# Two linear-attention blocks on one core: exp of q written and mixed in place, two relu buffers, the denominators' sums by two additions, places refitted

## The chip, the cores and the metric

The kernel runs on one core of one Trainium2 chip. A core has a matrix engine (PE, TensorE, with its weight loads PEld), a vector engine (DVE), a scalar engine (ACT), GpSimd (POOL) and SyncE (SP); SP and POOL issue the DMA transfers here. The engines run side by side, each through its own queue of instructions in the order in which the program gives them, and wait for one another by semaphores. The metric is the device time of one execution in microseconds (us); less is better.

## The reference

Two independent blocks, A and B, each on 2048 tokens of width 640 with 32 heads of 20, give their outputs side by side (2048 x 1280). Per block:

```
q, k, v = split(x @ wqkv)
phi(t)  = where(t > 0, t + 1, exp(t)) + 1e-6        # = min(exp(t), 1) + relu(t) + 1e-6
kv  = sum over tokens of phi(k) v^T   (per head)    z = sum over tokens of phi(k)
o   = (phi(q) kv) / (phi(q) z + 1e-6)               # per head
out = o @ wo
```

## The kernel before, in words

Everything is fp32. An fp32 product is made of three matmuls of rounded operands, high x high, high x low and low x high: a tile is *split* into a high part (ACT, a copy that rounds, L182) and a low part (DVE, the difference, L179).

**Phase 1 (to about 285 us)** makes the k half. phi(k) is needed for all tokens; instead of v, the Gram sums of phi(k) with x are formed and v's weights are applied to them afterwards (`kvmm`), and wo is applied to kv (`mmm`, and `m_step` for block B), which gives a matrix M per block so that the output is phi(q) M divided by the denominators. The large products are done in pairs by a scheme with seven products for eight (`product`, `combine`). Each pair has the seven products n = 0 to 6 in PSUM banks: n = 0, 2, 4, 5 use one bank `pa`, n = 1 and 6 `pe`, n = 3 `psb`. Products 2 and 5 add to or overwrite a bank which ACT must first have copied out (`ko<-pa` in phase 1, `o<-pa` in the q half, both L343).

**The q half (about 285 to 564 us)** goes through eight units u of 512 tokens, four per block. In unit u PE first runs `qmm(u, c)` for five chunks c of 128 features, 15 matmuls of 128x512 each into a bank `psq`, and then `outmm(u - 1)`: seven products for each of two halves, 108 matmuls of 128x320. For each chunk `qphi` makes phi(q): exp and relu on ACT (L950, L951), then the mix min(exp, 1) + relu on DVE (L952); `qacc` adds z times phi(q) into `acc`, on ACT for c = 0 and else on DVE (L962). When the chunks of a unit are done, `acc` holds, per token, the products that have to be summed over the rows of a head: `spread` (four SP transfers `da<-acc`) lays four groups of 32 partitions side by side, `invert` sums these four and takes the reciprocal on DVE, `gather` (four SP transfers `rd<-da`) brings it back to all 128 partitions, and `divide` (two halves, DVE, L1003) multiplies phi(q) by it. `d_sums`, `a_split` and `d_split` then make the operands of `outmm(u)` (`da` high and low, `ds` high and low). All this runs while PE works on `qmm(u + 1)`, since `outmm(u)` follows it.

**What sets the order.** Instructions are emitted in an order written by hand. In phase 1 each small piece of work is a job with a spot; `SHIFT` adds a number to a job's spot, and jobs are emitted by their spots. In the q half each piece is put at a slot: `("q", u, c, k)` is the place after the k-th group of three matmuls of chunk c, `("o", u, s)` the place after a product of `outmm(u)`; `AT` moves a piece by so many slots in that list. The high part of a split stands in its slot, and its low part follows one slot later. What is emitted first stands first in its engine's queue, and nothing behind it can pass.

Buffers: `pq` (phi(q) of a unit) has two, `eq` and `rq` one each, `rd` one.

Of the kernel before, what the change touches and what calls it, by code (L numbers as in the profile page):

```python
# [27 lines left out]
    ('fdh', 'k', 1, 6): 0.53, ('fdh', 'm', 0, 6): 0.52, ('fdh', 'm', 0, 7): 0.62, ('fdh', 'm', 0, 8): 0.57, ('fdl',  # L28
# [7 lines left out]
    ('gacc', 0, 1): 3.2, ('gacc', 1, 0): 2.35, ('gacc', 1, 3): 2.05, ('gacc', 2, 1): 2.89, ('gacc', 2, 3): 0.28,  # L36
    ('gacc', 3, 1): 2.86, ('gacc', 3, 2): 2.86, ('gacc', 3, 3): 3.83, ('gacc', 3, 5): 2.14, ('gacc', 4, 0): 0.75,
    ('gacc', 4, 4): 2.17, ('gacc', 5, 3): 1.28, ('gacc', 5, 5): 0.51, ('gacc', 6, 2): 0.82, ('gacc', 7, 0): 0.31,
# [5 lines left out]
    14): 4.05, ('mix', 15): -0.8, ('mix', 17): 1.76, ('mix', 19): 1.66, ('mix', 2): -0.07, ('mix', 20): 0.31,  # L44
    ('mix', 23): 0.53, ('mix', 26): 0.21, ('mix', 29): 2.2, ('mix', 3): -0.55, ('mix', 4): 7.31, ('mix', 5): 7.49,
# [17 lines left out]
    ('relu', 1): 0.93, ('relu', 10): 1.37, ('relu', 11): 0.09, ('relu', 13): 1.06, ('relu', 14): 1.59, ('relu', 21):  # L63
    4.46, ('relu', 25): 2.55, ('relu', 28): 1.48, ('relu', 30): 3.49, ('relu', 5): 1.82, ('s1', 10): -0.46, ('s1',
# [13 lines left out]
    ('woh', 4): -0.51, ('wol', 0): 0.5, ('wol', 3): 0.37, ('wol', 4): 0.03, ('wqh', 1): 2.01, ('wql', 2): -0.55,  # L78
# [43 lines left out]
def tile_linear_attn_pair(ctx: ExitStack, tc: tile.TileContext, ins, out: bass.AP):  # L122
# [863 lines left out]
    def invert(u):  # L986
        t = acc[u]
        nc.vector.tensor_reduce(t[:, 1, :P], t[:, 0].rearrange("p (j s) -> p s j", j=4),
                                axis=mybir.AxisListType.X, op=OP.add)
        nc.vector.reciprocal(t[:, 1, P:2 * P], t[:, 1, :P])  # L990
# [608 lines left out]
```

## Time and profile before

| what | value |
|---|---|
| median of 3 runs | 573.01 us (571.81 to 573.55) |
| the profiled execution's own time | 568.97 us |
| its span, first to last instruction | 567.2 us |
| granted TensorE clock | 1.000 |
| busy: PE, DVE, ACT, POOL | 559.9, 426.2, 329.9, 84.6 us |

A row of the timeline has the start in us, the duration, the engine, the line, the operation, out<-in by the program's names, the shapes, a count, and in brackets the time for which the engine stood idle before it and what ended that. A row of a group of instructions has the summed busy time and the mean ns of one, then the idle time of the engine before them. Matmuls are pipelined: the steps between their starts are the pace, and their durations overlap. A row of the waits has the total in us, the number of times and the longest.

### The profile page before, as it was taken

What the parts mean: (1) busy time and instruction counts of PE and PEld (TensorE: products, weight loads), DVE (VectorE), ACT (ScalarE), POOL (GpSimd) and SP (SyncE); (2) the same over time, 40 slices, a digit from 0 to 9 for tenths busy, and PEclk for the clock granted to TensorE, in tenths of its full rate; (3) what the DMA queues carried; (4) which work ended last, traced back from release to release, by engine and by line L of the source; (5) the groups of instructions that cost most, each with busy time, mean ns of one, the idle gap of its engine ahead of it and who ended that gap; (6) DMA issues with size and microseconds to landing.
All of it is one profiled execution on the core that took longest, in us unless ns stands there. A gap on an engine that the chain in (4) does not pass through costs nothing.

```text
span 567.2 us, 9114 instructions
## 1 busy us (share of the span) xinstructions
PE 559.9 (99%) x3231; PEld 511.5 (90%) x3231; DVE 426.2 (75%) x723; ACT 329.9 (58%) x619; POOL 84.6 (15%) x141
## 2 busy tenths in 40 slices
PE   8999999999999999999999999999999999999997
PEld 7989999898999898989888899898989989898997
DVE  5977799886585778887836895968679485776792
ACT  5964676663675775665736754646547354454551
POOL 0111122311011211242200103110012101001010
PEclk9999999999999999999999999999999999999999
DMA  8868689999885887999998976746466994432022
GB/s 281 242 155 245 169 239 298 288 315 356 304 206 141 199 259 135 353 226 297 319 266 282 333 249 237 253 130 215 153 214 226 305 366 145 155 94 102 1 94 92
DMA packets 78613, 126.74 MB, mean 223 GB/s; under 512 B 9768, under 2 KB 40872, under 8 KB 78568
## 3 DMA queue, kind: packets, MB, share of 16 engines
q1 hardware_dynamic: 66120, 86.28, 47.0%
q0 software_dynamic: 12160, 39.66, 25.6%
q8 instruction: 25, 0.41, 0.3%
q10 hardware_dynamic: 288, 0.23, 0.1%
q14 instruction: 20, 0.16, 0.1%
HBM read 73.62 MB, written 49.37 MB: 217 GB/s over the span
## 4 chain that ended last, share of the span: by engine, by line
PE 92%; DVE 3%; DMA 2%; ACT 1%; issue 0%; SPq 0%; ACTq 0%; DVEq 0%
PE pa L339 22%; PE pe L339 10%; PE psg L190 8%; PE psg L191 8%; PE psg L189 8%; PE psq L189 7%; PE psq L190 7%; PE psq L191 7%; PE psb L339 7%; PE psk L600 4%; PE pskv L782 2%; DMA wst<-in_A_wk 1%; DMA rd<-da 1%; PE psm L189 1%; PE psm L190 1%; PE psm L191 1%
## 5 line engine op out<-in xcount | busy, mean ns | idle before, releaser
L189 PE MATMUL psq<-xqh,wqh 128*128 128x512 f32 x200 | 78.4, 392 | 0.0
L191 PE MATMUL psq<-xqh,wql 128*128 128x512 f32 x200 | 78.0, 390 | 0.0
L190 PE MATMUL psq<-xql,wqh 128*128 128x512 f32 x200 | 77.9, 389 | 0.0
L189 PE MATMUL psg<-pkh,xnh 128*128 128x512 f32 x160 | 62.8, 393 | 0.0
L191 PE MATMUL psg<-pkh,xnl 128*128 128x512 f32 x160 | 62.7, 392 | 0.0
L190 PE MATMUL psg<-pkl,xnh 128*128 128x512 f32 x160 | 62.6, 392 | 0.0
L343 ACT ACTIVATE o<-pa 128x320 f32<-128x320 f32 x64 | 27.6, 440 | 49.7 <-PE pa L339 49.6
L567 POOL DMA_DIRECT2D zd<-ek x30 | 26.2, 873 | 140.1 <-DVE ek L559 50.1
L191 PEld LDWEIGHTS psq<-xqh,wql 128*128 128x128 f32 x200 | 37.5, 188 | 8.0
L190 PEld LDWEIGHTS psq<-xql,wqh 128*128 128x128 f32 x200 | 37.6, 188 | 7.3
L189 PEld LDWEIGHTS psq<-xqh,wqh 128*128 128x128 f32 x200 | 37.6, 188 | 7.2
L950 ACT ACTIVATE eq<-psq 128x512 f32<-128x512 f32 x40 | 23.8, 594 | 34.7 <-PE psq L191 26.2
L343 ACT ACTIVATE ko<-pa 128x320 f32<-128x320 f32 x52 | 22.5, 434 | 36.8 <-PE pa L339 36.6
L952 DVE SCALAR_TENSOR_TENSOR pq<-eq,rq 128x512 f32<-128x512 f32 x40 | 27.5, 688 | 12.4 <-ACT rq L951 12.2
L191 PEld LDWEIGHTS psg<-pkh,xnl 128*128 128x128 f32 x160 | 30.0, 188 | 6.5 <-DVE xnl L179 0.2
L1003 DVE SCALAR_TENSOR_TENSOR pq<-pq,rd 128x1280 f32<-128x1280 f32 x16 | 23.5, 1483 | 16.0 <-DMA rd<-da 16.0
L190 PEld LDWEIGHTS psg<-pkl,xnh 128*128 128x128 f32 x160 | 30.0, 188 | 5.8 <-DVE pkl L575 0.4
L189 PEld LDWEIGHTS psg<-pkh,xnh 128*128 128x128 f32 x160 | 30.0, 188 | 5.2
L571 ACT ACTIVATE pkh<-ek,epst 128x640 fp32r<-128x640 f32 x32 | 26.4, 832 | 11.5 <-DVE ek L559 11.4
L559 DVE SCALAR_TENSOR_TENSOR ek<-ek,ko 128x640 f32<-128x640 f32 x32 | 26.2, 820 | 7.8 <-ACT ko L556 6.8
L645 DVE TENSOR_TENSOR gacc<-psg,gacc 128x512 f32<-128x512 f32 (+2 forms) x42 | 25.6, 627 | 6.8 <-PE psg L191 6.5
L575 DVE SCALAR_TENSOR_TENSOR pkl<-ek,pkh 128x640 fp32r<-128x640 f32 x32 | 25.9, 819 | 6.0 <-ACT pkh L571 6.0
(212 smaller groups left out, 1657.7 us busy)
## 6 DMA issues: line engine op xcount, KB each, us to landing
zd<-ek POOLq DMA_DIRECT2D x32, 320.0 KB, 5.3
out<-o POOLq DMA_DIRECT2D x28, 320.0 KB, 3.6
xql<-xd SPq DMA_DIRECT2D x24, 256.0 KB, 4.0
xt<-in_B_xt_tiles SPq DMA_DIRECT2D x16, 320.0 KB, 5.0
xn<-in_B_x SPq DMA_DIRECT2D x16, 320.0 KB, 5.7
xqs<-in_A_xt SPq DMA_DIRECT2D x20, 256.0 KB, 5.8
xqs<-in_B_xt SPq DMA_DIRECT2D x20, 256.0 KB, 6.2
fdmh<-fsh POOLq DMA_DIRECT2D x14, 320.0 KB, 4.5
```

The costliest lines, as they stand in the source:

```text
L189: nc.tensor.matmul(o, whi, xhi, start=first, stop=False)
L190: nc.tensor.matmul(o, whi, xlo, start=False, stop=False)
L191: nc.tensor.matmul(o, wlo, xhi, start=False, stop=last)
L339: nc.tensor.matmul(o, x, y, start=start and m == r == 0, stop=m == len(terms) - 1 and r == 2, skip_group_check=True)
L343: nc.scalar.activation(x, y, AF.Copy)
L559: nc.vector.scalar_tensor_tensor(ek[n], ek[n], 1.0, rk[n], op0=OP.min, op1=OP.add)
L567: nc.gpsimd.dma_start(zacc[b], e, accum_op=OP.add)
L571: nc.scalar.activation(pk[n][0], ek[n], AF.Identity, bias=epst)
L575: nc.vector.scalar_tensor_tensor(lo, ek[n], EPS, f32(hi), op0=OP.add, op1=OP.subtract)
L645: nc.vector.tensor_tensor(o, x, o, op=OP.add)
L950: nc.scalar.activation(e, ps, AF.Exp)
L952: nc.vector.scalar_tensor_tensor(pq[u][:, c, :], e, 1.0, r, op0=OP.min, op1=OP.add)
```

## The change

Three edits in the code and two in its tables of places.

- `qphi`: exp writes into the chunk of `pq` itself and the mix works there in place; the tile `eq` is gone. `rq` has two buffers. So the exp of a chunk waits no longer for the mix of the chunk before it, which read `eq`; the relu waits for the mix two chunks back.
- `invert`: the reduction over four columns becomes two additions, of 256 and of 128 columns. The reciprocal is the same; `gather` reads it from another place of the same tile.
- `AT` is written anew: about half of its entries have other values, some are new, some gone. From `SHIFT` 24 entries are taken out, so that these jobs go back to the spots that they have without it (among them ('mix', 17), the mix of a token group of phase 1).

```
 SHIFT = {
...
-    14): 4.05, ('mix', 15): -0.8, ('mix', 17): 1.76, ('mix', 19): 1.66, ('mix', 2): -0.07, ('mix', 20): 0.31,
...
+    14): 4.05, ('mix', 15): -0.8, ('mix', 19): 1.66, ('mix', 2): -0.07, ('mix', 20): 0.31, ('mix', 23): 0.53,
...
 AT = {
-    ('a_split', 1, 0): 3, ('a_split', 2, 0): 3, ('a_split', 3, 0): -1, ('a_split', 3, 1): 2, ('a_split', 5, 0): -2,
...
+    ('d_split', 1, 0): 7, ('d_split', 1, 1): 5, ('d_split', 3, 1): -5, ('d_sums', 1, 0): 4, ('divide', 1, 0): 1,
...
+    'm', 1, 2): -3, ('form_split', 'm', 1, 3): -11, ('form_split', 'm', 1, 8): 3, ('form_split', 'm', 1, 9): 5,
+    ('form_sums1', 'm', 1, 1): -5, ('gather', 5): 4, ('invert', 3): -1, ('invert', 5): 3, ('kv_step', 1, 5): -2,
+    ('load_w', 'q', 1, 0): -3, ('load_w', 'q', 1, 4): 8, ('m_step', 1, 2): 1, ('m_step', 1, 3): 1, ('split_o', 1,
...
     def qphi(u, c, ps):
...
-        e = q2[0].tile([P, 512], F32, name="eq", tag="eq", bufs=1)
-        r = q1a[0].tile([P, 512], F32, name="rq", tag="rq", bufs=1)
+        e = pq[u][:, c, :]
+        r = q1a[0].tile([P, 512], F32, name="rq", tag="rq", bufs=2)
         nc.scalar.activation(e, ps, AF.Exp)
         nc.scalar.activation(r, ps, AF.Relu)
-        nc.vector.scalar_tensor_tensor(pq[u][:, c, :], e, 1.0, r, op0=OP.min, op1=OP.add)
+        nc.vector.scalar_tensor_tensor(e, e, 1.0, r, op0=OP.min, op1=OP.add)
...
     def invert(u):
         t = acc[u]
-        nc.vector.tensor_reduce(t[:, 1, :P], t[:, 0].rearrange("p (j s) -> p s j", j=4),
-                                axis=mybir.AxisListType.X, op=OP.add)
-        nc.vector.reciprocal(t[:, 1, P:2 * P], t[:, 1, :P])
+        tt = nc.vector.tensor_tensor
+        tt(t[:, 1, :2 * P], t[:, 0, :2 * P], t[:, 0, 2 * P:], op=OP.add)
+        tt(t[:, 1, 2 * P:3 * P], t[:, 1, :P], t[:, 1, P:2 * P], op=OP.add)
+        nc.vector.reciprocal(t[:, 1, 3 * P:], t[:, 1, 2 * P:3 * P])
...
     def gather(u):
...
-            nc.sync.dma_start(r[32 * j:32 * (j + 1), :], t[:, 1, P:2 * P])
+            nc.sync.dma_start(r[32 * j:32 * (j + 1), :], t[:, 1, 3 * P:])
```

The line numbers of the changed kernel are 5 or 6 lower than before.

The order of DVE in unit 2, from the last operation on z (`zs`) to the first low part `dsl` that `outmm(1)` reads, and beyond; before:

```order
L751 TENSOR_SCALAR zs<-zs 128x1
L179 TENSOR_TENSOR dsl<-sr,dsh 128x1024
L179 TENSOR_TENSOR fsl<-wst,fsh 128x640
L952 SCALAR_TENSOR_TENSOR pq<-eq,rq 128x512
L962 SCALAR_TENSOR_TENSOR acc<-pq,z,acc 128x512
L179 TENSOR_TENSOR dal<-pq,dah 128x768
L179 TENSOR_TENSOR dal<-pq,dah 128x256
```

and after the change:

```order
L745 TENSOR_SCALAR zs<-zs 128x1
L173 TENSOR_TENSOR fsl<-wst,fsh 128x640
L946 SCALAR_TENSOR_TENSOR pq<-pq,rq 128x512
L956 SCALAR_TENSOR_TENSOR acc<-pq,z,acc 128x512
L173 TENSOR_TENSOR dal<-pq,dah 128x768
L173 TENSOR_TENSOR dal<-pq,dah 128x256
L173 TENSOR_TENSOR dsl<-sr,dsh 128x1024
```

The first `dsl` has moved behind a weight's low part, a mix, an accumulation and the second `dal`.

The order of ACT in the same unit, from the exp of the fourth chunk to the first copies out of the product bank; before:

```order
L950 ACTIVATE eq<-psq 128x512
L951 ACTIVATE rq<-psq 128x512
L886 ACTIVATE fsh<-wst 128x640
L182 ACTIVATE dsh<-sr 128x1024
L950 ACTIVATE eq<-psq 128x512
L951 ACTIVATE rq<-psq 128x512
L343 ACTIVATE o<-pa 128x320 x3
```

and after the change:

```order
L944 ACTIVATE pq<-psq 128x512
L945 ACTIVATE rq<-psq 128x512
L176 ACTIVATE dsh<-sr 128x1024
L944 ACTIVATE pq<-psq 128x512
L945 ACTIVATE rq<-psq 128x512
L337 ACTIVATE o<-pa 128x320
L880 ACTIVATE fsh<-wst 128x640
L337 ACTIVATE o<-pa 128x320 x2
```

The rounding of a weight (`fsh`) has moved from between the last two exps to behind the first copy.

In phase 1, ACT at about 153 us, where block A's tenth pair of products is on PE and the first `kvmm` steps stand between its products; before:

```order
L343 ACTIVATE ko<-pa 128x320
L547 ACTIVATE ek<-ko 128x640
L556 ACTIVATE ko<-ko 128x640
L435 ACTIVATE kah<-xt 128x512
L343 ACTIVATE ko<-pa 128x320
L571 ACTIVATE pkh<-ek,epst 128x640
```

and after the change:

```order
L337 ACTIVATE ko<-pa 128x320
L565 ACTIVATE pkh<-ek,epst 128x640
L541 ACTIVATE ek<-ko 128x640
L550 ACTIVATE ko<-ko 128x640
L429 ACTIVATE kah<-xt 128x512
L337 ACTIVATE ko<-pa 128x320
```

`pkh`, which reads what the mix (17) has written, now stands ahead of the exp, the relu, the rounding and the second copy out of `pa`. On DVE that mix has moved ahead of two low parts of x (`xnl`).

More of the change, by code (lines that the diff above doesn't have):

```diff
@@ L27 @@
     0, 0): 0.42, ('f5', 'k', 0): -0.1, ('f5', 'k', 1): -2.28, ('fdh', 'k', 1, 2): 0.51, ('fdh', 'k', 1, 4): 0.91,
-    ('fdh', 'k', 1, 6): 0.53, ('fdh', 'm', 0, 6): 0.52, ('fdh', 'm', 0, 7): 0.62, ('fdh', 'm', 0, 8): 0.57, ('fdl',
[7 rows of a table removed]
-    ('gacc', 0, 1): 3.2, ('gacc', 1, 0): 2.35, ('gacc', 1, 3): 2.05, ('gacc', 2, 1): 2.89, ('gacc', 2, 3): 0.28,
-    ('gacc', 3, 1): 2.86, ('gacc', 3, 2): 2.86, ('gacc', 3, 3): 3.83, ('gacc', 3, 5): 2.14, ('gacc', 4, 0): 0.75,
-    ('gacc', 4, 4): 2.17, ('gacc', 5, 3): 1.28, ('gacc', 5, 5): 0.51, ('gacc', 6, 2): 0.82, ('gacc', 7, 0): 0.31,
+    ('fdh', 'k', 1, 6): 0.53, ('fdh', 'm', 0, 7): 0.62, ('fdh', 'm', 0, 8): 0.57, ('fdl', 'k', 1, 1): 0.84, ('fdl',
[6 rows of a table added]
+    ('fl', 'm', 0, 8): 1.99, ('gacc', 0, 1): 3.2, ('gacc', 1, 0): 2.35, ('gacc', 1, 3): 2.05, ('gacc', 2, 1): 2.89,
+    ('gacc', 2, 3): 0.28, ('gacc', 3, 1): 2.86, ('gacc', 3, 2): 2.86, ('gacc', 3, 3): 3.83, ('gacc', 3, 5): 2.14,
+    ('gacc', 4, 0): 0.75, ('gacc', 4, 4): 2.17, ('gacc', 5, 3): 1.28, ('gacc', 5, 5): 0.51, ('gacc', 7, 0): 0.31,
     ('gacc', 7, 1): 0.04, ('gacc', 7, 4): 0.45, ('gacc', 7, 5): 1.7, ('gacc', 7, 6): 2.69, ('iota', 0): 0.8, ('kt',
@@ L43 @@
     ('ld', 'm', 0, 4): -0.19, ('mc', 4, 1): 0.69, ('mix', 11): 0.24, ('mix', 12): 0.49, ('mix', 13): 7.61, ('mix',
-    14): 4.05, ('mix', 15): -0.8, ('mix', 17): 1.76, ('mix', 19): 1.66, ('mix', 2): -0.07, ('mix', 20): 0.31,
-    ('mix', 23): 0.53, ('mix', 26): 0.21, ('mix', 29): 2.2, ('mix', 3): -0.55, ('mix', 4): 7.31, ('mix', 5): 7.49,
[17 rows of a table removed]
-    ('relu', 1): 0.93, ('relu', 10): 1.37, ('relu', 11): 0.09, ('relu', 13): 1.06, ('relu', 14): 1.59, ('relu', 21):
-    4.46, ('relu', 25): 2.55, ('relu', 28): 1.48, ('relu', 30): 3.49, ('relu', 5): 1.82, ('s1', 10): -0.46, ('s1',
[13 rows of a table removed]
-    ('woh', 4): -0.51, ('wol', 0): 0.5, ('wol', 3): 0.37, ('wol', 4): 0.03, ('wqh', 1): 2.01, ('wql', 2): -0.55,
[19 rows of a table removed]
+    14): 4.05, ('mix', 15): -0.8, ('mix', 19): 1.66, ('mix', 2): -0.07, ('mix', 20): 0.31, ('mix', 23): 0.53,
+    ('mix', 26): 0.21, ('mix', 29): 2.2, ('mix', 3): -0.55, ('mix', 5): 7.49, ('mix', 7): 1.18, ('mix', 8): 4.49,
[16 rows of a table added]
+    11): 0.09, ('relu', 13): 1.06, ('relu', 21): 4.46, ('relu', 25): 2.55, ('relu', 28): 1.48, ('relu', 30): 3.49,
[13 rows of a table added]
+    ('wol', 4): 0.03, ('wqh', 1): 2.01, ('wql', 2): -0.55, ('wql', 4): 2.4, ('xh', 10, 'A1'): -0.17, ('xh', 10,
[17 rows of a table added]
 }
@@ L106 @@
 AT = {
-    ('a_split', 1, 0): 3, ('a_split', 2, 0): 3, ('a_split', 3, 0): -1, ('a_split', 3, 1): 2, ('a_split', 5, 0): -2,
-    ('a_split', 6, 0): 6, ('d_split', 1, 1): 5, ('d_split', 2, 1): -2, ('d_split', 5, 0): 2, ('d_split', 5, 1): 5,
-    ('d_sums', 1, 0): 3, ('d_sums', 3, 0): 1, ('d_sums', 5, 0): -1, ('divide', 1, 0): 1, ('divide', 1, 1): 1,
-    ('divide', 2, 0): 3, ('divide', 2, 1): 2, ('form_last', 'm', 1): 2, ('form_split', 'm', 1, 0): 2, ('form_split',
-    'm', 1, 1): -2, ('form_split', 'm', 1, 2): -1, ('form_split', 'm', 1, 3): -4, ('form_split', 'm', 1, 5): -5,
-    ('form_split', 'm', 1, 8): 2, ('form_split', 'm', 1, 9): 4, ('form_sums1', 'm', 1, 1): -6, ('gather', 6): 3,
-    ('invert', 3): -1, ('invert', 6): -4, ('kv_step', 1, 2): 1, ('kv_step', 1, 5): -2, ('load_w', 'q', 1, 4): 9,
-    ('m_step', 1, 3): 1, ('split_o', 1, 4): -1, ('split_w', 1, 0): -3, ('split_w', 1, 2): -10, ('split_w', 1, 4): 2,
-    ('z_turn', 1): 2,
+    ('a_split', 1, 0): 2, ('a_split', 2, 0): -1, ('a_split', 3, 0): -1, ('a_split', 5, 0): 2, ('a_split', 6, 0): 7,
+    ('d_split', 1, 0): 7, ('d_split', 1, 1): 5, ('d_split', 3, 1): -5, ('d_sums', 1, 0): 4, ('divide', 1, 0): 1,
+    ('divide', 2, 0): 1, ('divide', 5, 0): 1, ('form_last', 'm', 1): 5, ('form_load', 0, 5): -2, ('form_load', 1,
+    1): -2, ('form_load', 1, 5): -1, ('form_split', 'm', 1, 0): 5, ('form_split', 'm', 1, 1): -4, ('form_split',
+    'm', 1, 2): -3, ('form_split', 'm', 1, 3): -11, ('form_split', 'm', 1, 8): 3, ('form_split', 'm', 1, 9): 5,
+    ('form_sums1', 'm', 1, 1): -5, ('gather', 5): 4, ('invert', 3): -1, ('invert', 5): 3, ('kv_step', 1, 5): -2,
+    ('load_w', 'q', 1, 0): -3, ('load_w', 'q', 1, 4): 8, ('m_step', 1, 2): 1, ('m_step', 1, 3): 1, ('split_o', 1,
+    5): -2, ('split_w', 1, 0): -3, ('split_w', 1, 2): -7, ('split_w', 1, 4): 1,
 }
```

108 rows, old and new, of the table SHIFT are left out of this document.

## The prediction

> **What bounds the kernel now.** I read the page's first part first: busy time by engine.
>
> ```profile
> PE 559.9 (99%) x3231; PEld 511.5 (90%) x3231; DVE 426.2 (75%) x723; ACT 329.9 (58%) x619; POOL 84.6 (15%) x141
> ```
>
> PE is busy for 559.9 of 567.2 us. The change takes no matmul away, so it can win only where PE stands still or runs slower than its pace. Second view: the waits of PE, and beside them the one kind of wait of ACT that the new tile and buffers touch (us in total, times, longest).
>
> ```profile
> PE pa L339 <- ACT o L343: 2.0, 2, 1.0
> ```
>
> ```profile
> ACT eq L950 <- DVE pq L952: 7.0, 8, 1.8
> ```
>
> Two waits of PE, 2.0 us together, are for ACT's copy of a half product (`o<-pa`): the third product of outmm writes a bank that is free only when the first product has been copied out of it. And ACT waits 7.0 us in eight places until the mix has read `eq`. Third view: the instructions of PE at these two waits.
>
> ```profile
> 364.53 0.40 PE L191 MATMUL psq<-xqh,wql 128*128 128x512 f32 x1
> 364.77 0.31 PE L339 MATMUL pa<-fh,dah 128*128 128x320 f32 x1
> ...
> 368.14 0.31 PE L339 MATMUL pe<-fh,dsl 128*128 128x320 f32 x1
> 369.48 0.41 PE L339 MATMUL pa<-fh,dsh 128*128 128x320 f32 x1 [1.03 <-ACT o L343]
> ```
>
> ```profile
> 468.07 0.31 PE L339 MATMUL pe<-fh,dsl 128*128 128x320 f32 x1
> 469.32 0.42 PE L339 MATMUL pa<-fh,dsh 128*128 128x320 f32 x1 [0.94 <-ACT o L343]
> ```
>
> From 364.77 to 368.14 are 24 matmuls, 23 steps: 3.37 / 23 = 0.147 us each. The step to 369.48 is 1.34, so 1.19 is lost, and the matmul after the wait takes 0.41 instead of 0.31, another 0.10: **1.29 us** at unit 2. By the same sum unit 5 loses 1.25 - 0.147 + 0.10 = **1.20 us**. These 2.49 us are what can be won in the q half. From the copy's start to the matmul that it frees I take 0.50 in both places (368.98 to 369.48, 468.82 to 469.32, rows below).
>
> **Part 1: exp into pq, two buffers for relu.** ACT's rows ahead of the two late copies:
>
> ```profile
> 365.42 0.60 ACT L950 ACTIVATE eq<-psq 128x512 f32<-128x512 f32 x1 [1.82 <-DVE pq L952]
> ...
> 368.01 0.60 ACT L950 ACTIVATE eq<-psq 128x512 f32<-128x512 f32 x1
> ...
> 368.98 0.78 ACT L343 ACTIVATE o<-pa 128x320 f32<-128x320 f32 x2
> ```
>
> ```profile
> 462.73 0.60 ACT L950 ACTIVATE eq<-psq 128x512 f32<-128x512 f32 x1 [1.25 <-DVE pq L952]
> ...
> 465.69 0.60 ACT L950 ACTIVATE eq<-psq 128x512 f32<-128x512 f32 x1
> ...
> 467.85 0.60 ACT L950 ACTIVATE eq<-psq 128x512 f32<-128x512 f32 x1 [1.07 <-DVE pq L952]
> ...
> 468.82 0.77 ACT L343 ACTIVATE o<-pa 128x320 f32<-128x320 f32 x2
> ```
>
> In time, the copy must start 0.50 ahead of the step that PE would take: at 368.14 + 0.15 - 0.50 = 367.79 in unit 2, and at 467.72 in unit 5. It starts 0.97 after the last exp (368.01 to 368.98), with the relu between.
>
> Unit 5: if nothing but the wait of 1.07 goes, the last exp starts at 466.78 and the copy at 467.75, on the edge. The wait of 1.25 ahead of it goes too, since ACT then waits only for the mix two chunks back, so 1.2 us come on top. Gain **1.20**, the whole stall; what bounds it is 1.10 (edge missed by a little) to 1.20.
>
> Unit 2: the wait of 1.82 goes, and the weight rounding (`fsh`) that stood between the last two exps is now behind the copy, as the order shows. The last exp then starts when its bank is full, after the matmul of 364.53 has ended at 364.93; say 364.97. Copy at 365.94, 1.85 ahead of its time. Gain **1.29**, if the next operand is there (part 3). Costs: no instruction is added. A mix that writes where it reads needs a price; the nearest rows are operations of the k half of the same shapes, one in place and one not.
>
> ```profile
> L559 DVE SCALAR_TENSOR_TENSOR ek<-ek,ko 128x640 f32<-128x640 f32 x32 | 26.2, 820 | 7.8 <-ACT ko L556 6.8
> ...
> L575 DVE SCALAR_TENSOR_TENSOR pkl<-ek,pkh 128x640 fp32r<-128x640 f32 x32 | 25.9, 819 | 6.0 <-ACT pkh L571 6.0
> ```
>
> 820 and 819 ns: in place costs nothing. The rest of the eight waits, 2.9 of the 7.0 us, stands where no copy is late, or chunks ahead of a copy; it gives nothing by itself.
>
> **Part 2: the sums of the denominators.** The groups that price it, and the one taken away:
>
> ```profile
> L453 DVE TENSOR_TENSOR sx<-sx,xt 128x256 f32<-128x256 f32 x13 | 5.5, 426 | 0.4
> ...
> L179 DVE TENSOR_TENSOR kal<-xt,kah 128x128 fp32r<-128x128 f32 x16 | 4.5, 283 | 0.0
> ```
>
> ```profile
> L988 DVE TENSOR_REDUCE da<-da 128x128 f32<-128x512 f32 x6 | 6.5, 1085 | 5.5 <-DMA da<-acc 5.5
> ```
>
> One 1.085 is replaced by 0.426 + 0.283 = 0.71, with one more handing on between dependent instructions, some 0.04: 0.33 us less, six times. The Trainium skill ("VectorE: DVE Perf Modes", Rules for kernel authors) says to keep the number of DVE operations down, since each pays for emptying the pipe; its formula for the fp32 add, (N + 151) / 0.96 ns, gives 0.42 and 0.29 us, which the rows bear out, and also 0.16 us for the fixed part, so that by the rule alone, with as many elements read, the pair would be 0.16 slower and not 0.33 faster, and the sum at the end -1.1 instead of -1.6. The row of the reduction, twice as long as four operands of 128 take, decides for the pair. The 0.33 is worth nothing by itself: DVE idles in every unit until `rd` lands. It counts through the landing only, in unit 2.
>
> **Part 3: the places in unit 2.** DVE there:
>
> ```profile
> 353.08 2.90 DVE L1003 SCALAR_TENSOR_TENSOR pq<-pq,rd 128x1280 f32<-128x1280 f32 x2 [3.93 <-DMA rd<-da]
> ...
> 360.69 0.69 DVE L952 SCALAR_TENSOR_TENSOR pq<-eq,rq 128x512 f32<-128x512 f32 x1
> 361.41 0.75 DVE L962 SCALAR_TENSOR_TENSOR acc<-pq,z,acc 128x512 f32<-128x512 f32 x1
> 362.08 0.18 DVE L747 TENSOR_REDUCE z<-zr 128x5 f32<-128x20 f32 x1
> ...
> 362.77 1.22 DVE L179 TENSOR_TENSOR dsl<-sr,dsh 128x1024 fp32r<-128x1024 f32 x1
> 363.90 0.82 DVE L179 TENSOR_TENSOR fsl<-wst,fsh 128x640 fp32r<-128x640 f32 x1
> 364.64 0.69 DVE L952 SCALAR_TENSOR_TENSOR pq<-eq,rq 128x512 f32<-128x512 f32 x1
> ...
> 366.03 1.29 DVE L179 TENSOR_TENSOR dal<-pq,dah 128x768 fp32r<-128x768 f32 x2
> 367.23 0.68 DVE L952 SCALAR_TENSOR_TENSOR pq<-eq,rq 128x512 f32<-128x512 f32 x1
> ```
>
> ```profile
> 366.68 0.19 PEld L339 LDWEIGHTS pe<-fh,dsl 128*128 128x128 f32 x1
> ```
>
> From the divide on, DVE works without a gap. The first `dsl` is done at 363.99 and wanted by PE's weight load at 366.68. Afterwards four things stand ahead of it: `fsl` (363.90 to 364.64: 0.74), a mix (360.69 to 361.41: 0.72), an accumulation (361.41 to 362.08: 0.67) and two `dal` (366.03 to 367.23: 1.20), 3.33 together. It starts at 362.77 + 3.33 = 366.10 and ends at 367.32. With the divide 0.33 sooner: 366.99, and PE loads at 367.02: 0.34 late, and 0.10 for the slow first matmul. **Loss 0.44**. Bounds: 0 (`rd` lands 0.7 sooner) and 0.77 (the 0.33 does not pass through the transfers). I take 0.44 because the gather is issued as soon as the reciprocal is done, so that an earlier end is an earlier issue.
>
> In the other units I followed both queues in the same way: the first copy is there 1.4 to 1.8 us ahead of need, since exp and relu of the last chunk (0.97) are all that stands between the full bank and the copy, and `dsl` 2 us ahead or more. The places of `invert` and `gather` in units 5 to 7 move the landing of `rd` by up to 1 us inside that margin: nothing. SP's queue keeps its sequence in the q half but for two pairs of loads that swap. The step of M that now stands behind three more matmuls (`m_step`, 1, 2) adds none: nothing.
>
> **Part 4: phase 1, without 24 shifts.** Most of them put an instruction before or after a neighbour with a wide margin. One place has a narrow one, at 153 to 157 us, where `pkh` now stands ahead of an exp, a relu, a `kah` and the copy that PE's sixth product waits for:
>
> ```profile
> 152.73 0.82 DVE L179 TENSOR_TENSOR xnl<-xn,xnh 128x640 fp32r<-128x640 f32 x1
> ```
>
> ```profile
> 153.54 0.73 ACT L547 ACTIVATE ek<-ko 128x640 f32<-128x640 f32 x1
> 154.30 0.74 ACT L556 ACTIVATE ko<-ko 128x640 f32<-128x640 f32 x1
> 154.95 0.62 ACT L435 ACTIVATE kah<-xt 128x512 fp32r<-128x512 f32 x1
> 155.59 0.44 ACT L343 ACTIVATE ko<-pa 128x320 f32<-128x320 f32 x1
> 155.92 0.82 ACT L571 ACTIVATE pkh<-ek,epst 128x640 fp32r<-128x640 f32 x1
> 156.64 0.29 ACT L795 ACTIVATE kvh<-kvt 120x120 fp32r<-120x120 f32 x1
> ```
>
> ```profile
> 156.36 0.39 PE L339 MATMUL pa<-wfh,kah 128*128 128x320 f32 x1
> ```
>
> The mix takes the place of `xnl` at 152.73 and is done at 153.55; `pkh` starts at 153.58, 0.04 after the exp's old start, and takes 0.72 (155.92 to 156.64). So all behind it comes 0.76 later, the copy at 156.35, the matmul at 156.85 instead of 156.36: **loss 0.49**. Bounds: 0 (if ACT is earlier here) and 0.9 (0.76 and a slow first matmul, no slack).
>
> **Sum:** -1.29 - 1.20 + 0.44 + 0.49 = **-1.56 us** against the profiled execution's 568.97. The median of the runs is 573.01, 4.0 longer; I let that distance stand: 573.01 - 1.56 = 571.4, or -0.27%. What a measurement of this kernel can tell from no change is about 0.3%, 1.7 us, so that this forecast lies at the edge.
>
> **Rivals.** (a) The two new waits don't come: `rd` of unit 2 lands sooner, and ACT has slack at 154. For it: the landing of `rd` varies, and in unit 2, where DVE waits 3.93 for it, it is one of the slow ones (the view of the tile `rd`, 24 transfers, us from issue to landing, min, median, max):
>
> ```profile
> DMA to landing us min/median/max: 2.2/2.7/5.0
> ```
>
> Then -2.49 or, where the runs lose more at these stalls than the profile shows, -3.5: 570.5 to 569.5. (b) In unit 2 the wait for the copy is only exchanged for one for `dsl`: DVE's row is full from 353.08 on, and every us that `rd` comes later counts whole. One us later: -1.56 + 1.0, 572.4. Against it: 5.0 is already the slowest landing. (c) Slower: the same late `dsl`, decided by the landing of `rd`. The stores of split weights at that time go out in another sequence, and if these fill the DMA engines in the few us after `invert`, `rd` waits behind them; from 3.3 us later on, the whole is slower by over 0.3% (3.6: 575.0). The median landing of 2.7 and the maximum of 5.0 speak against it. To this I count a place of phase 1 that I priced at nothing.
>
> **How the numbers follow.** The forecast has 0.60, and with 0.5 us for the runs' own spread a little under half of it lies beyond -0.3%; (a) 0.20, (b) 0.08, (c) 0.12. Faster: 0.28 + 0.20 = 0.48; same: 0.32 + 0.08 = 0.40; slower 0.12. The range goes from (a) with its larger loss, 569.5, to both new waits at their bounds (-2.49 + 0.77 + 1.0 for an `rd` one us late + 0.9 = +0.18) and 0.5 for the spread, 573.7.
>
> **What would show it.** After the change PE has no wait for `o<-pa` of over 0.1 us, and ACT none for the mix in units 2 and 5. PE waits about 0.3 us for `dsl` in the first `pe` product of unit 2, and its step at 156 us is about 0.5 longer. The pair of additions starts 0.79 us ahead of the reciprocal. The prediction is wrong if a wait for `o<-pa` stays, if `rd` of unit 2 lands over a us from 352.7, or if PE stands still in phase 1 anywhere else than before.

## The result

| | before | after |
|---|---|---|
| median of 9 runs each | 571.81 us (569.91 to 574.63) | 567.85 us (566.94 to 569.45) |
| ratio, 95% interval | | 0.993 [0.9905, 0.9956] |
| the profiled execution's own time | 568.97 us | 567.32 us |
| its span | 567.2 us | 565.2 us |

The change makes the kernel 0.7% faster. The direction was forecast, the size not: 571.4 us stood against a median of 573.01, a ratio of 0.997, with a range down to 569.5. On another chip the medians of the same two kernels lie 3.4 us apart (570.87 and 567.46). The two profiled executions lie only 1.65 us apart (2.0 in span), the medians 4.0. How that can be is the main question below.

The waits of PE after the change (total in us, times, longest), the whole answer of that view:

```profile
PE psi L1111 <- DVE idle L1108: 1.0, 1, 1.0
PE pa L333 <- ACT mev L337: 0.7, 1, 0.7
```

Both waits for `o<-pa` are gone, and no wait at all is left in the q half. The place in unit 2 where PE stood for 1.03 us at 369.48, on PE and ACT after the change:

```profile
368.68 0.31 PE L333 MATMUL pe<-fh,dsl 128*128 128x320 f32 x1
368.83 0.31 PE L333 MATMUL pa<-fh,dsh 128*128 128x320 f32 x1
```

```profile
365.51 0.60 ACT L944 ACTIVATE pq<-psq 128x512 f32<-128x512 f32 x1 [1.23 <-PE psq L185]
366.00 0.59 ACT L945 ACTIVATE rq<-psq 128x512 f32<-128x512 f32 x1
366.48 0.44 ACT L337 ACTIVATE o<-pa 128x320 f32<-128x320 f32 x1
```

The step is 0.15, the pace. The last exp now waits for its bank to be filled (PE) and no longer for a mix (DVE), and the copy follows 0.97 behind it, as worked out. DVE and the weight load that were to be late:

```profile
352.51 2.89 DVE L998 SCALAR_TENSOR_TENSOR pq<-pq,rd 128x1280 f32<-128x1280 f32 x2 [2.80 <-DMA rd<-da]
...
365.53 1.22 DVE L173 TENSOR_TENSOR dsl<-sr,dsh 128x1024 fp32r<-128x1024 f32 x1
```

```profile
367.22 0.19 PEld L333 LDWEIGHTS pe<-fh,dsl 128*128 128x128 f32 x1
```

`dsl` is done at 366.75 and loaded at 367.22: 0.47 in hand instead of 0.34 late. The sums on DVE:

```profile
344.42 0.41 DVE L983 TENSOR_TENSOR da<-da 128x256 f32<-128x256 f32 x1
344.86 0.29 DVE L984 TENSOR_TENSOR da<-da 128x128 f32<-128x128 f32 x1
345.19 0.95 DVE L985 RECIPROCAL da<-da 128x128 f32<-128x128 f32 x1
```

The reciprocal starts 0.77 behind the first addition; 1.12 it was behind the reduction. And the place of phase 1 that the prediction priced:

```profile
155.22 1.21 PE L776 MATMUL pskv<-gacc,wv 128*120 128x120 f32 x10
156.54 0.41 PE L333 MATMUL pa<-wfh,kah 128*128 128x320 f32 x1
```

From the ten small matmuls to the sixth product it takes 1.32 now; before it was 0.98 (155.38 to 156.36).

### The profile page after: what moved, and what is told of

Its sections match the earlier page's. It is cut to its first block, busy times and chain, and to the rows that moved or that the text cites. A ratio compares the mean times of both kernels' runs of the same rounds, so it can differ in the third digit from the quotient of the medians.

```text
span 565.2 us, 9089 instructions
## 1 busy us (share of the span) xinstructions
PE 560.1 (99%) x3231; PEld 512.0 (91%) x3231; DVE 423.8 (75%) x729; ACT 329.5 (58%) x619; POOL 84.4 (15%) x141
## 4 chain that ended last, share of the span: by engine, by line
PE 96%; ACT 1%; DMA 1%; issue 0%; DVE 0%; POOL 0%; DVEq 0%; ACTq 0%
PE pa L333 22%; PE pe L333 11%; PE psq L183 8%; PE psq L185 8%; PE psq L184 8%; PE psg L184 8%; PE psg L185 8%; PE psg L183 8%; PE psb L333 7%; PE psk L594 5%; PE pskv L776 2%; DMA md<-mev 1%; PE psi L1111 1%; PE psm L183 1%; PE psm L185 1%; PE psm L184 1%
## 5 line engine op out<-in xcount | busy, mean ns | idle before, releaser
L944 ACT ACTIVATE pq<-psq 128x512 f32<-128x512 f32 x40 | 23.7, 594 | 28.0 <-PE psq L185 27.8
L946 DVE SCALAR_TENSOR_TENSOR pq<-pq,rq 128x512 f32<-128x512 f32 x40 | 27.4, 686 | 8.4 <-ACT rq L945 8.4
L340 DVE TENSOR_TENSOR o<-pe,o 128x320 f32<-128x320 f32 x32 | 15.3, 479 | 20.4 <-PE pe L333 13.5
```

What stands on the lines that cost most here:

```text
L944: nc.scalar.activation(e, ps, AF.Exp)
L946: nc.vector.scalar_tensor_tensor(e, e, 1.0, r, op0=OP.min, op1=OP.add)
```

## The experiments

Theories at the start. **A**: the kernel before loses a varying time at the copies out of the product bank, because the landing of `rd` varies; the in-place exp alone takes that away. **B**: the extra length of its runs lies elsewhere. **C**: the new places gain. After the first runs came **D** (edits and new places are both needed), **F** (the two edits of the code together are enough) and **G** (the denominators make a loop from unit to unit). All ratios are to the kernel before on the same chip, with 95% intervals.

**The kernel before, another execution of it.** No edit.

> The kernel before, unchanged, for another profiled execution of it. Theory A (the kernel before loses a varying time at the copies out of the product bank, because the landing of rd varies and the exps wait for the mixes): this profile differs from the first; PE's waits for o<-pa sum to something other than 2.0 us, and where the execution is longer than 568.97 by x us, these waits are longer by most of x, with rd landing later in the units concerned. Theory B (the extra length of the runs lies elsewhere: the start, the end, phase 1): the waits for o<-pa stay at 2.0 +-0.3 us and the difference stands at other lines. Ratio to the kernel before: 1.000 within its interval.

Ratio 1.0006 [0.9989, 1.0023]. The profiled execution took 570.86 us, 1.89 more than the first, near the median of its runs (570.73). Its wait of PE for the copies, and the one that the first execution did not have:

```profile
PE pa L339 <- ACT o L343: 2.6, 3, 1.1
```

```profile
436.18 0.31 PE L339 MATMUL pe<-fh,dsl 128*128 128x320 f32 x1
437.31 0.41 PE L339 MATMUL pa<-fh,dsh 128*128 128x320 f32 x1 [0.82 <-ACT o L343]
```

This is unit 4. The exp ahead of that copy had been released by PE in the first execution; in this one, 2.1 us later, it is released by a mix (first execution, then this one):

```profile
433.76 0.60 ACT L950 ACTIVATE eq<-psq 128x512 f32<-128x512 f32 x1 [1.29 <-PE pa L339]
```

```profile
435.84 0.60 ACT L950 ACTIVATE eq<-psq 128x512 f32<-128x512 f32 x1 [1.29 <-DVE pq L952]
```

By the steps between the starts of PE's matmuls (0.147 for 320 columns, 0.227 for 512, all that is over the pace added up), this execution loses 3.4 us in the q half, the first one 2.5. The other 1 us lies in phase 1: PE's first `psq` matmul, the start of the q half, stands at 286.04 in the first execution and at 286.98 in this one. So theory A holds for half of the difference and B for the other half, and the first profile was an execution with little waiting.

**Exp in place and two relu buffers alone**, all places and the reduction as before:

```
-        e = q2[0].tile([P, 512], F32, name="eq", tag="eq", bufs=1)
-        r = q1a[0].tile([P, 512], F32, name="rq", tag="rq", bufs=1)
+        e = pq[u][:, c, :]
+        r = q1a[0].tile([P, 512], F32, name="rq", tag="rq", bufs=2)
...
-        nc.vector.scalar_tensor_tensor(pq[u][:, c, :], e, 1.0, r, op0=OP.min, op1=OP.add)
+        nc.vector.scalar_tensor_tensor(e, e, 1.0, r, op0=OP.min, op1=OP.add)
```

> The kernel before with one edit: exp into pq, mix in place, two buffers for relu; all places and the reduction as before. Theory A: both waits for o<-pa are gone, since the last exp no longer waits for a mix; profiled PE time lost falls by about 2.5 us, and the runs gain as much as the whole change or nearly: -3 to -4 us (0.993 to 0.995). Theory C (the new places are what gains): -1 us or less (0.998 to 1.000).

Ratio 1.0002 [0.998, 1.0024]: nothing that can be measured. Two of the twelve executions weigh on this ratio: 575.20 and 572.50 us, with a mean granted clock of 0.994 and 0.997. The medians alone (569.65 against 570.31) give 0.9988, 0.7 us. The waits for `o<-pa` are gone as theory A says, and another has come, twice:

```profile
PE pe L339 <- DVE o L346: 2.1, 2, 1.0
```

The first of them, on DVE and on PE:

```profile
409.86 1.09 DVE L988 TENSOR_REDUCE da<-da 128x128 f32<-128x512 f32 x1 [2.98 <-DMA da<-acc]
410.98 0.95 DVE L990 RECIPROCAL da<-da 128x128 f32<-128x128 f32 x1
411.85 0.43 DVE L346 TENSOR_TENSOR o<-pe,o 128x320 f32<-128x320 f32 x1
```

```profile
410.99 0.31 PE L339 MATMUL pa<-f,dal 128*128 128x320 f32 x1
412.33 0.41 PE L339 MATMUL pe<-fh,dsh 128*128 128x320 f32 x1 [1.04 <-DVE o L346]
```

The seventh product of outmm writes the bank `pe`, which the addition `o<-pe` must first have read. That addition stands in DVE's queue behind the sum of the denominators, and the sum waits 2.98 us for `da` to land. PE loses 1.19 in that step, and again at 447.82 in the next unit. The forecast of theory A falls: the time won at the copies is given back there. The reason is in one more row of each kernel, the divide that runs during unit 3 (of unit 2's phi(q)); before, then with the exp in place:

```profile
383.52 2.90 DVE L1003 SCALAR_TENSOR_TENSOR pq<-pq,rd 128x1280 f32<-128x1280 f32 x2 [0.92 <-DMA rd<-da]
```

```profile
383.46 2.89 DVE L1003 SCALAR_TENSOR_TENSOR pq<-pq,rd 128x1280 f32<-128x1280 f32 x2 [1.86 <-DMA rd<-da]
```

PE is 1.0 us further in the second one (the last `psq` matmul of unit 3 starts at 397.69, before at 398.69), `rd` is not. The denominators go round once per unit: `da` lands, sum, `rd` lands, divide, DVE's queue of the unit, `acc`, `da` again. Where this loop is late, it stops PE at one or the other of the two waits.

**The changed kernel with the old qphi** (the four lines above turned back in the changed kernel):

> The changed kernel with the eq tile and one relu buffer back (old qphi), additions and all new places kept. Theory A: waits for o<-pa in units 2 and 5 come back, 1 to 3 us in sum, and the runs stand at -1 to +1 us against the kernel before (0.998 to 1.002). Theory C: -3 us or more (0.995 or below).

Ratio 1.001 [0.9989, 1.0032]. The wait for `o<-pa` is back, not in units 2 and 5 as expected but in one place, unit 4:

```profile
435.22 0.31 PE L333 MATMUL pe<-fh,dsl 128*128 128x320 f32 x1
437.81 0.46 PE L333 MATMUL pa<-fh,dsh 128*128 128x320 f32 x1 [2.28 <-ACT o L337]
```

Ahead of the copy stands an exp that has waited 2.64 us for a mix:

```profile
436.34 0.60 ACT L944 ACTIVATE eq<-psq 128x512 f32<-128x512 f32 x1 [2.64 <-DVE pq L946]
```

This execution, 572.24 us, is the second longest of twelve (median 569.78), and it pays for more than the wait. The granted clock reads 0.80 from 435 to 440 us, 0.85 from 440 to 445, and 1.00 before and after. From 437.81 to 441.50 there are 14 steps of 0.26 us on the average, where the pace is 0.147: another 1.6 us. Theory C falls: additions and new places without the in-place exp gain nothing.

**The additions alone:**

```
-        nc.vector.tensor_reduce(t[:, 1, :P], t[:, 0].rearrange("p (j s) -> p s j", j=4),
-                                axis=mybir.AxisListType.X, op=OP.add)
-        nc.vector.reciprocal(t[:, 1, P:2 * P], t[:, 1, :P])
+        tt = nc.vector.tensor_tensor
+        tt(t[:, 1, :2 * P], t[:, 0, :2 * P], t[:, 0, 2 * P:], op=OP.add)
+        tt(t[:, 1, 2 * P:3 * P], t[:, 1, :P], t[:, 1, P:2 * P], op=OP.add)
+        nc.vector.reciprocal(t[:, 1, 3 * P:], t[:, 1, 2 * P:3 * P])
...
-            nc.sync.dma_start(r[32 * j:32 * (j + 1), :], t[:, 1, P:2 * P])
+            nc.sync.dma_start(r[32 * j:32 * (j + 1), :], t[:, 1, 3 * P:])
```

> The kernel before with one edit: the two additions in place of the reduction. By the prediction's own rows the divide of units 2 and 5 starts 0.33 us sooner, so that both late copies are 0.33 us less late: -0.6 to -0.7 us (0.999). If the landing of rd is set by other transfers and not by its issue, 0.

Ratio 1.0004 [0.9989, 1.002]. In the profile the two late copies are less late, by about as much as forecast:

```profile
PE pa L339 <- ACT o L343: 1.4, 2, 0.7
```

1.4 instead of 2.0. The runs cannot tell 0.6 us from nothing.

**The changed kernel itself, again:**

> The changed kernel itself, for its ratio on this chip and a second profiled execution: 0.993 (0.9905 to 0.9956 before). No wait of PE for o<-pa or o<-pe of over 0.3 us in the q half.

Ratio 0.9937 [0.9915, 0.9958]; its second profile (567.07 us) has no wait in the q half either.

**The changed kernel with the old AT table:** the whole table `AT` as before, both edits kept.

> The changed kernel with the places of the q half (AT) as before the change; both edits of the code and the shortened SHIFT kept. Theory D (two waits hang on the late denominators: the exp for the mix, and PE's sixth bank for the o<-pe addition which stands behind the sums that wait for da; the in-place exp takes the first away, the places the second): the second wait stays, at 409 to 412 or 443 to 448 us, 1 to 2.5 us in all, and the runs stand at 0.998 to 1.001. Theory F (the two edits of the code together are the gain): 0.993 to 0.995.

Ratio 0.9944 [0.9926, 0.9963], no wait in the q half. Theory D falls and F stands: the refitted places, the larger part of the diff, are worth nothing that can be measured. In the traces they do one thing that the prediction did not see. PE wants `dsl` of unit 2 behind a longer queue with the new `AT`, but `rd` of unit 2 lands sooner with it. From the first issue of `rd` to the divide it takes 7.12 to 7.22 us in all ten profiles with the old `AT`, and 6.27 to 6.39 in all five with the new one; SP's rows of the kernel before and of the changed kernel, whose divides start at 353.08 and 352.51:

```profile
345.93 2.59 SPq L996 DMA_DIRECT2D rd<-da  x4
```

```profile
346.17 2.59 SPq L991 DMA_DIRECT2D rd<-da  x4
```

The stores that POOL issues at that time stand in another sequence with the new `AT`; that this is the cause was not tested. A trace of use in the times there may be: 5 of these 12 runs lie at 568.65 to 568.90, the other 7 at 566.64 to 567.40, while the 8 runs of the changed kernel beside them end at 568.13; but the changed kernel's first runs reached 569.45, so that this use is not shown.

**The changed kernel with the old SHIFT table:** all 24 entries back.

> The changed kernel with the whole SHIFT of before. By the prediction the wait at 156 us goes (0.3 us less than in the changed kernel) and nothing else moves: 0.992 to 0.994. If the 24 entries carry the gain: 0.996 or more.

Ratio 0.9931 [0.9906, 0.9955]: no difference from the changed kernel, as expected. The wait at 156 us is gone, but the wait for `mev` at 196 us is 1.0 in its profile, where the two of the changed kernel have 0.7 and 0.5.

**Exp in place, and the sums of units 3 and 4 put behind the additions** (on the kernel before with exp in place; of `AT` the entries that change):

```
+    ('gather', 3): 2, ('gather', 4): 2,
-    ('invert', 3): -1,
+    ('invert', 3): 2, ('invert', 4): 2,
```

> The kernel before with exp in place and two relu buffers, and the sums of the denominators of units 3 and 4 (with their gathers) moved two or three places, behind the two o<-pe additions of the fifth product. Theory D: the two waits of PE for o<-pe of the run with exp in place alone (1.0 each) are gone, no wait for o<-pa returns, and the runs gain 2 to 3 us: 0.994 to 0.997. If the late da or rd is only handed on, a wait of about 1 us turns up elsewhere: 0.998 to 1.000.

Ratio 0.994 [0.9917, 0.9963], and the q half has no wait. Nothing is made shorter here; the addition `o<-pe` only no longer stands behind an instruction that waits for a transfer:

```profile
409.27 0.49 DVE L346 TENSOR_TENSOR o<-pe,o 128x320 f32<-128x320 f32 x1
409.68 1.07 DVE L988 TENSOR_REDUCE da<-da 128x128 f32<-128x512 f32 x1
```

**Both edits of the code, every place as before** (the two diffs above together on the kernel before):

> The kernel before with both edits of the code (exp in place with two relu buffers, and the two additions), every place of before. Theory G (the denominators make a loop from unit to unit: da lands, sums, rd lands, divide, DVE's queue of the next unit, acc, da again; PE waits where this loop runs late, and the edits each shorten it by a few tenths up to the point where no wait is left): no wait for o<-pa, and the waits for o<-pe of the run with exp in place alone are gone or under 0.7 us in all; 0.994 to 0.996. If the additions' 0.33 us count only for themselves: two waits of about 0.7 stay, 0.998 to 0.999.

Ratio 0.9948 [0.9933, 0.9963]. So the additions, worth nothing alone, are worth about 3 us on top of the exp in place (1.0002 to 0.9948). The profiled execution was one of the two longest of six (568.46) and has one wait left for `o<-pe`, 0.36 us at 446.92. Against the run with the exp alone, unit 3 reads (exp alone, then both):

```profile
397.69 0.40 PE L191 MATMUL psq<-xqh,wql 128*128 128x512 f32 x1
```

```profile
403.84 1.26 SPq L983 DMA_DIRECT2D da<-acc  x2
```

```profile
398.76 0.40 PE L191 MATMUL psq<-xqh,wql 128*128 128x512 f32 x1
```

```profile
404.17 1.26 SPq L983 DMA_DIRECT2D da<-acc  x2
```

```profile
409.42 0.43 DVE L989 TENSOR_TENSOR da<-da 128x256 f32<-128x256 f32 x1 [1.48 <-DMA da<-acc]
```

Measured from PE's last `psq` matmul, the first `da` is issued 0.74 sooner (5.41 behind it instead of 6.15), the sums start 5.25 after that instead of 6.02, 0.77 less, and they take 0.33 less up to the addition `o<-pe`: 1.84 us against the 1.19 that the seventh product was late. Of these, 0.33 is the edit itself; the 0.74 fits the loop, where a unit's start inherits what the unit before saved: the divide during unit 3 already starts 0.71 sooner against that matmul (383.82 against 398.76, 383.46 against 397.69); for the landing no cause is shown.

**Exp in place, and unit 3's da ahead of the xql loads** (on the kernel before with exp in place). SP issues the five loads of the next unit's low parts of x in front of the four `da` transfers; here behind them (the new entries of `AT`):

```
+    ('load_xq', 4, 0): 7, ('load_xq', 4, 1): 6, ('load_xq', 4, 2): 5, ('load_xq', 4, 3): 4, ('load_xq', 4, 4): 3,
```

> The kernel before with exp in place and two relu buffers, and unit 3's four da transfers issued ahead of the five xql loads of the next unit on SP's queue (these loads moved 3 to 7 places back); the order on DVE, ACT and PE is that of the run with exp in place alone, except that nothing else moves. Theory G: da of unit 3 lands 2 us or more sooner than at 409.86, the wait of 1.0 at 411 us goes, rd of unit 4 lands sooner by as much and the wait of 1.0 at 446 us shrinks to under 0.5: 0.994 to 0.997. If the late da is not what PE waits for: as the run with exp in place alone, 0.998 to 1.001.

Ratio 0.9941 [0.9929, 0.9954], no wait in the q half, on a kernel whose DVE order is that of the run which gained nothing. SP's queue and DVE:

```profile
401.84 2.56 SPq L983 DMA_DIRECT2D da<-acc  x4
404.52 2.87 SPq L274 DMA_DIRECT2D xql<-xd  x5
```

```profile
406.71 1.07 DVE L988 TENSOR_REDUCE da<-da 128x128 f32<-128x512 f32 x1
```

The transfers are issued 2.0 sooner, and the sum starts 3.15 sooner, with no wait for them. Both waits for `o<-pe` are gone, the one of unit 4 too, where nothing was moved: there the first `da` is issued 5.29 us after PE's last `psq` matmul (435.77 and 430.48), with the exp alone it was 7.91 (439.77 and 431.86). So what unit 3 gains is handed on to unit 4, as theory G has it. Two experiments by different means, this one and the one with the sums behind the additions, show the cause: the late `da` of unit 3 and the sum that waits for it ahead of `o<-pe`.

**Both edits, and the sums of units 3 and 4 behind the additions:**

> The kernel before with both edits of the code and the sums of units 3 and 4 with their gathers behind the two o<-pe additions. Theory G: no wait in the q half, and none of the longer executions that the changed kernel still has: 0.992 to 0.995, with the runs closer together.

Ratio 0.9943 [0.9931, 0.9955], six runs between 566.71 and 567.27. Not faster than the changed kernel: with no wait left in the q half, nothing there is to be won.

**Unit 3's da first, without any edit of the code** (the same five entries on the kernel before):

> The kernel before with one move: unit 3's da transfers ahead of the five xql loads; exp, relu and sums as before. Theory G with two loops: the wait for o<-pa of unit 2 (1.0 to 1.3) stays, since nothing ahead of it is moved; rd of unit 4 lands about 2 us sooner, so the wait of unit 4 (0.8 in one execution of before) goes and that of unit 5 (0.7 to 0.9) shrinks or goes: 0.996 to 0.998. If the in-place exp is not needed at all: 0.994 and no wait for o<-pa.

Ratio 0.9959 [0.9942, 0.9975]. The waits of PE:

```profile
PE pa L339 <- ACT o L343: 1.2, 2, 1.0
```

1.00 of it is unit 2, which the move cannot reach, 0.23 unit 5; unit 4 has none. The profiled execution, 570.47 us, is the longest of its seven (median 568.26); it starts the q half at 288.30, 2.3 us later than the first execution of before. By the ratios, five numbers in a table give about two thirds of what the whole change gives, but the intervals (0.25 to 0.58% against 0.42 to 0.85% in the changed kernel's second measurement) leave the share open. The wait of unit 2 is what is left for the in-place exp: the same move together with it has none.

**The changed kernel with ('mix', 17) back in SHIFT:**

> The changed kernel with one entry of SHIFT back, ('mix', 17). By the prediction the step of PE at 156 us, 0.45 to 0.5 longer than pace in the changed kernel, falls back to under 0.2, and the rest of the program is as in the changed kernel; in time 0.3 us, which the runs cannot tell: 0.992 to 0.995.

Ratio 0.9931 [0.9916, 0.9947]. The step at 156 us is at its old length:

```profile
155.33 1.21 PE L776 MATMUL pskv<-gacc,wv 128*120 128x120 f32 x10
156.31 0.39 PE L333 MATMUL pa<-wfh,kah 128*128 128x320 f32 x1
```

But in this profile PE waits 0.85 us at 209.28 and 0.27 at 233.66 for copies of phase 1, where the changed kernel's first profile had 0.66 at 197.22. That the time won at 156 us is lost again at a later wait for that reason is not shown: waits at 196, 209 and 233 us come and go from execution to execution, with the old `SHIFT` too.

## Why the prediction was wrong

The forecast was -1.56 us; the medians gave -4.0 in the first measurement and -3.4 on another chip. Its sum, -1.29 - 1.20 + 0.44 + 0.49, failed in all its terms: the two late copies (-2.49) were priced too low, and the two losses (+0.93) did not come. Besides, the median of the kernel before was 571.81 over nine runs where the sum started from 573.01; this makes 1.2 us of the distance between 571.4 and 567.85 and is no fault of the reasoning.

- **Part 1, the two late copies: right about the waits, wrong about what they are worth alone.** Both waits are gone, in every execution profiled with the in-place exp, and in the changed kernel the copy of unit 2 follows 0.97 behind an exp that waits for its bank. But the 2.49 us were credited to this edit, and by itself it gains nothing that can be measured (1.0002).
- **"I let that distance stand": the step that failed most.** The sum was made against one execution with 2.5 us of such loss, and the 4.0 us up to the median were taken for something that the change doesn't touch. The second execution of the kernel before, at its median, loses 3.4 us in the q half, with a third late copy in unit 4 (0.82), which the first had just escaped. The changed kernel loses nothing there in either execution. So the term of the late copies, -2.49, was -3.4 in a middling execution.
- **Part 3, the loss of 0.44 for dsl in unit 2: did not come.** `rd` came 1.11 us sooner against PE, not 0.33 (352.51 - 365.31 against 353.08 - 364.77, from the divide to the first matmul of outmm). Some 0.8 of this is the shorter time from the issue of `rd` to the divide (6.34 instead of 7.15). This is not the varying landing that rival (a) supposed: it goes with the new `AT` in every profile, while the prediction saw in the changed sequence of the stores only a way for `rd` to come later (rival (c)). The DVE queue itself ran as worked out: 13.02 from the start of the divide to the start of `dsl` (352.51 to 365.53) where the forecast had 13.02 (353.08 to 366.10).
- **Part 2, "worth nothing by itself ... through the landing only, in unit 2": right alone, wrong together.** Alone the additions give 1.0004. With the in-place exp they decide whether the loop keeps up with PE: 1.0002 without, 0.9948 with. The size of the saving was right: 0.35 against 0.33.
- **What the forecast did not see at all** is why the in-place exp by itself gains nothing. It followed DVE's queue as if it stood still in time while PE moved forward; but a PE that no longer waits in units 2 and 5 comes earlier to every later wait. In the first execution of before, the `o<-pe` addition behind the sum of unit 3 starts at 410.70 and the seventh product at 412.13; the addition must start 0.48 ahead of it, so there were 0.95 us of slack. With the exp alone the addition starts 1.15 later and PE wants it 0.99 sooner: 1.19 too late. That the direction came out right is in part luck: both edits were made together, and the prediction had no reason why they need each other.
- **Part 4, 0.49 at 156 us: the wait is there, the loss cannot be found.** The step is 0.34 longer (1.32 against 0.98). Taking it away changes no median that the runs can tell apart. The start of the q half, which holds all that phase 1 loses, differs more from execution to execution (286.04 to 288.30 in the ten profiles with the old `SHIFT`) than between the tables (286.41 to 287.10 in the five others, one of them with one entry back).
- **Rivals.** (a) came nearest in size, with its larger loss of 3.5 us at the late copies, but its reasons held only in part: `rd` landed sooner because of the change's own places, and ACT had too little slack at 154. (b) and (c), a `dsl` that grows late, did not show; the late transfer they feared turned up in another place, as the late `da` in front of `o<-pe`.

With the terms as measured: -3.4 for the q half and 0 for phase 1 give 571.81 - 3.4 = 568.4 us; measured 567.85. The 0.5 us between them stay open; on the other chip -3.4 is the whole difference.

## What to carry to other kernels

When a wait is taken away, the engine that waited comes earlier to all later ones: follow the loop that feeds it (here denominators, once per unit) and ask whether it comes earlier too, or whether only the place of the wait changes. An instruction that waits for a transfer should not stand ahead of one for which the bound engine waits; moving it back by two or three places, or issuing the transfer ahead of loads that are not yet wanted, was worth as much here, with the exp in place, as the two additions (0.994 each, against 0.9948). One profiled execution is one draw: where its time is below that of the other runs, as here, its margins of a tenth of a us must be priced as waits.

## What the runs showed of the hardware

- Two additions of 256 and 128 columns (0.41 and 0.29 us) and their handing on take 0.77; the strided reduction from 512 to 128 columns takes 1.08, start to start 1.12. The Trainium skill ("VectorE: DVE Perf Modes", Rules for kernel authors) has the advice not to spend more operations than needed, and also that `tensor_reduce` is the slowest; this case agrees with the second.
- A mix that writes where it reads, and that works on a tile in which ACT writes another chunk, takes as long as one with a tile of its own: 686 ns against 688, in 40 instructions each.
- The same four small transfers (`da` of unit 3), issued on the same queue behind five larger loads, take 4.4 to 6.0 us from the first issue to the sum, in the eleven profiles where the sum waits for them. Issued ahead of these loads they land 4.1 and 4.2 us after the first issue (two profiles). The DMA engines were 0.78 to 0.92 busy meanwhile in the first case and 0.5 in the second, but among the eleven the busier ones were not the slower ones: 6.0 us at 0.78, 4.4 at 0.92. That spread, over a us, is as large as the waits that this change removes.
- The longest standstill of PE in these profiles, 2.28 us in the changed kernel with the old qphi, was followed by 3.4 us in which the granted clock was halved. After the waits of the other fourteen profiles, 1.55 us at the most, no such drop stands in the trace while the program runs. One case does not show the cause.
